# Storing two output tiles with one DMA in place of four, all on the sync queue

## The chip, the cores and the metric

The kernel runs on one core of a Trainium2 chip. The metric is the device time of one execution in microseconds (us), taken outside the profiler's page; the span that a profile shows is some 1.8 us shorter. Lower is better. Runs of one kernel scatter by about 2%; a run more than 1.5% above the fastest of its kernel is called slow. Medians below are over all runs, slow ones too; ratios are over fast runs alone.

## The reference

```python
def sm_attn(qq, kk, vv):
    s = scale * np.matmul(qq, kk.transpose(0, 1, 3, 2))
    a = np.exp(s - np.max(s, axis=-1, keepdims=True))
    a = a / (np.sum(a, axis=-1, keepdims=True) + 1e-09)
    return np.matmul(a, vv)
p_packed = sm_attn(p, k, v)              # q, k, v: (8, 8, 576, 64); p: (8, 8, 32, 64)
attn = sm_attn(q, p_packed, p_packed)
x = attn.transpose(0, 2, 1, 3).reshape(8, 576, 512)
W_tok = scale * np.einsum('bsd,btd->bst', x @ w_q, x @ w_k)
out = np.maximum(np.einsum('bst,btd->bsd', W_tok, x), 0.0) @ w_out     # (8, 576, 512) fp32
```

## The kernel before

Everything is written out as a fixed order of steps for each engine. Loads of q, k and v (fp32 in memory, bf16 on chip) go through the GpSimd queue, but for the k of the first batch, which the scalar and sync queues carry. An output tile has 128 rows: partition `s * 32 + g` holds token `18 * g + 8 * tp + 2 * s + e`, where `e` tells the two tiles of a pair apart. So for one `s`, 32 partitions hold 32 rows of memory that are 18 tokens apart, and with both tiles of a pair each of them writes 4 KB in one piece. The old code issues one DMA for each `s`:

```python
        o = new("o", (b, tp), [P, 2, D], fp32, "o", opool)          # five buffers
        copy(eng, o[:, t % 2, x:x + w], T["ot", b, t, x])
        done[b, tp] = done.get((b, tp), 0) + w
        if done[b, tp] == 2 * D:
            dst = out[b].rearrange("(g r) n -> g (r n)", r=RQ)[:, tp * 4096:(tp + 1) * 4096]
            for s in range(4):
                queue = nc.scalar if w < D and s % 2 else nc.sync   # scalar: last pair alone
                queue.dma_start(dst[:, s * 1024:(s + 1) * 1024],
                                o[s * GQ:(s + 1) * GQ].rearrange("a e n -> a (e n)"))
```

A remainder of 64 rows for two batches goes out in one DMA (`o_rem`), on the sync queue, the last one on the GpSimd queue.

The softmax here doesn't subtract the row's maximum and nothing guards it: scores larger than these inputs give would overflow.

## Time and profile before

| | before |
|---|---|
| time, median | 124.64 us (123.6 to 126.11, 3 runs, before the change was timed) |
| span of the profiled run | 122.5 us |
| PE busy | 106.5 us, 87% |
| mean DMA rate (as counted on landing) | 208 GB/s |
| output stores | 64 of 128 KB, 4 remainders of 256 KB |
| last load landed | 91.5 us |
| last output tile evacuated | 113.45 us |

The prediction shows the lines of the page that carry this. In those of section 2 (slices) each digit is a fortieth of the span, in tenths of busy time. In the table by stretches, a row is the stretch, its length, the busy time of each engine with the number of instructions, then the TensorE clock granted, the DMA share and GB/s. The DMA queues q0 and q1 carry the loads of the GpSimd queue and the DMAs of the sync queue.

### The profile page before, as it was taken

Reading aid. Unit: us, or ns where it says so; the run is one execution under the profiler, and the core shown is the slowest. Engines: PE = TensorE matmul, PEld = TensorE weight load, DVE = VectorE, ACT = ScalarE, POOL = GpSimd, SP = SyncE. Lnnn points to the kernel's source line nnn. Section 1 sums busy time; section 2 is a strip of 40 time slices with the busy share of each in tenths; the row PEclk is TensorE's granted clock in tenths of the full one; section 3 lists DMA queues with packets and bytes.
Section 4 is the critical chain, followed back from the end, with each engine's and each line's share of the span. In section 5 each row is a group of like instructions: output and inputs, shape, how many; then the busy total and the mean of one; then the engine's idle time right before and its main releaser. Section 6 shows DMA issues by size and latency. Waiting matters only on the chain.

```text
span 122.5 us, 4561 instructions
## 1 busy us (share of the span) xinstructions
PE 106.5 (87%) x1968; PEld 70.1 (57%) x1968; DVE 81.3 (66%) x197; ACT 78.2 (64%) x159; POOL 37.9 (31%) x49
## 2 busy tenths in 40 slices
PE   6989989687999999999998999989999989998000
PEld 2576746565748757568585657766585646354000
DVE  6362456667876858598864689987996988754000
ACT  3131568766779798799858888678767866464000
POOL 6949302722059004757000066600070120000200
PEclk9999999999999999999999999999999999999755
DMA  3999999999999999999999999999972526782584
GB/s 67 373 157 186 195 213 206 209 207 206 213 208 211 269 298 217 243 212 262 303 224 208 220 289 283 267 274 273 202 157 79 130 64 185 213 211 67 152 226 135
DMA packets 16485, 25.47 MB, mean 208 GB/s; under 512 B 3168, under 2 KB 11360, under 8 KB 16464
## 3 DMA queue, kind: packets, MB, share of 16 engines
q0 software_dynamic: 11872, 14.68, 68.9%
q1 hardware_dynamic: 4224, 9.64, 25.7%
q10 hardware_dynamic: 368, 0.85, 2.6%
q8 instruction: 15, 0.25, 0.7%
q14 instruction: 6, 0.05, 0.1%
HBM read 30.15 MB, written 9.44 MB: 323 GB/s over the span
## 4 chain that ended last, share of the span: by engine, by line
PE 52%; issue 16%; DVE 11%; DMA 7%; POOL 4%; ACT 3%; POOLq 1%; ACTq 0%
PE out_ps L518 14%; DMA q_sb<-in_q_dram 7%; PE qT_ps L369 6%; PE pv_ps L328 6%; PE aT_ps L423 3%; PE kT_ps L280 3%; PE e_ps L310 3%; PE e_ps L388 3%; PE mix_ps L486 2%; PE wkq_ps L444 2%; DVE kT L134 2%; DVE a L414 2%; DVE rs L404 2%; POOL wqk L169 2%; PE wkq_ps L439 2%
## 5 line engine op out<-in xcount | busy, mean ns | idle before, releaser
L414 POOL TENSOR_TENSOR a<-e,rr 128x512 bf16<-128x512 f32 (+1 forms) x12 | 15.0, 1258 | 55.2 <-DVE rr L408 34.0
L518 PE MATMUL out_ps<-wout,relu 128*128 128x512 bf16 (+1 forms) x132 | 31.4, 373 | 0.0
L518 PEld LDWEIGHTS <-relu 128*128 128x128 bf16 x132 | 11.7, 98 | 10.6 <-issue 0.4
L130 ACT ACTIVATE o<-out_ps 128x512 f32<-128x512 f32 (+1 forms) x21 | 12.3, 587 | 5.5 <-PE out_ps L518 3.8
L316 ACT ACTIVATE e<-e_ps 128x512 bf16<-128x512 f32 (+1 forms) x24 | 11.0, 490 | 7.1 <-PE e_ps L310 7.0
L404 DVE TENSOR_REDUCE rs<-e 128x16 f32<-128x512 f32 (+1 forms) x16 | 12.9, 809 | 3.2 <-ACT e L397 2.7
L397 ACT ACTIVATE e<-e_ps 128x512 f32<-128x512 f32 (+1 forms) x24 | 11.5, 524 | 4.3 <-PE e_ps L388 4.0
L134 DVE COPY o<-out_ps 128x512 f32<-128x512 f32 (+1 forms) x12 | 8.0, 664 | 5.9 <-PE out_ps L518 4.9
L496 ACT ACTIVATE relu<-mix_ps 128x512 bf16<-128x512 f32 x19 | 10.3, 600 | 1.7 <-PE mix_ps L486 1.1
L498 DVE TENSOR_SCALAR relu<-mix_ps 128x512 bf16<-128x512 f32 x13 | 8.6, 682 | 3.3 <-PE mix_ps L486 3.3
L369 PE MATMUL qT_ps<-idb,q_sb 128*64 128x128 bf16 x288 | 10.7, 220 | 0.1
L130 ACT ACTIVATE qT<-qT_ps 128x1024 bf16<-128x1024 bf16 (+1 forms) x13 | 9.3, 736 | 0.3 <-PE qT_ps L369 0.3
L559 PE MATMUL warm_ps<-warm 128*128 128x512 bf16 x26 | 8.5, 463 | 1.2 <-DVE warm L137 1.2
L369 PEld LDWEIGHTS <-q_sb 128*64 128x64 bf16 x288 | 8.7, 110 | 1.2 <-issue 0.7
L130 ACT ACTIVATE kT<-kT_ps 128x1024 bf16<-128x1024 bf16 (+2 forms) x10 | 7.3, 755 | 2.1 <-PE kT_ps L286 2.1
L388 PE MATMUL e_ps<-ppT,qT 128*128 128x64 bf16 x160 | 7.8, 193 | 0.8 <-issue 0.5
L423 PE MATMUL aT_ps<-idb,a 128*128 128x128 bf16 x80 | 7.3, 220 | 1.4 <-issue 0.7
L328 PE MATMUL pv_ps<-v_sb,e 64*64 64x192 bf16 x288 | 8.3, 246 | 0.0
L388 PEld LDWEIGHTS <-qT 128*128 128x128 bf16 x160 | 6.4, 98 | 3.0 <-issue 1.8
L134 DVE COPY qT<-qT_ps 128x1024 bf16<-128x1024 bf16 (+1 forms) x11 | 6.6, 603 | 2.1 <-PE qT_ps L369 2.1
L310 PE MATMUL e_ps<-pdiag,kT 128*64 128x64 bf16 x288 | 7.6, 197 | 0.4 <-DVE kT L134 0.2
L444 PE MATMUL wkq_ps<-aT,pqk 128*128 128x256 bf16 (+1 forms) x64 | 7.7, 233 | 0.0
(84 smaller groups left out, 192.5 us busy)
## 6 DMA issues: line engine op xcount, KB each, us to landing
out_dram<-o SPq DMA_DIRECT2D x62, 128.0 KB, 4.7
q_sb<-in_q_dram POOLq DMA_DIRECT2D x8, 576.0 KB, 15.2
v_sb<-in_v_dram POOLq DMA_DIRECT2D x8, 576.0 KB, 15.7
k_sb<-in_k_dram POOLq DMA_DIRECT2D x7, 576.0 KB, 17.1
out_dram<-o_rem SPq DMA_DIRECT2D x3, 256.0 KB, 5.9
k<-in_k_dram ACTq DMA_DIRECT2D x1, 576.0 KB, 4.3
k<-in_k_dram SPq DMA_DIRECT2D x1, 576.0 KB, 6.9
wout<-in_moe_w_out_dram POOLq DMA_DIRECT2D x2, 256.0 KB, 19.9
```

The costliest lines, as they stand in the source:

```text
L130: nc.scalar.activation(o, i, COPY)
L134: nc.vector.tensor_copy(o, i)
L310: nc.tensor.matmul(ps[halves(i), at[0]:at[1] + 1:at[1] - at[0]], T["kT", b][:, place(b, m), halves(i)], rhs, start=True, stop=True)
L316: nc.scalar.activation(e1[:, 2 * z0:2 * z1], T["s1", b, c], EXP, scale=scale)
L328: nc.tensor.matmul(T["pv", b][i][halves(cc)], lhsT, rhs, start=n == 0, stop=n == R - 1, skip_group_check=True)
L369: nc.tensor.transpose(ps[halves(x), z - z0], q_in[b][:, x, r * Dh:(r + 1) * Dh], idb)
L388: nc.tensor.matmul(ps[:, t - 2 * c, i, cc], lhsT, T["ppT", b][:, i, cc], start=True, stop=True)
L397: nc.scalar.activation(e2(b, min(c, 1))[:, o:o + n], T["s2", b, c].rearrange("a t i c (x l) -> a (t i c x) l", l=L), EXP, scale=scale)
L404: e.tensor_reduce(rs, T["e2", (b, d)], axis=AX, op=ADD)
L414: e.tensor_tensor(a2[:, 2 * d:2 * d + n].rearrange("a t i (u l) -> a (t i u) l", l=L), T["e2", (b, d)], T["rr", (b, d)].to_broadcast((P, n ...
L423: nc.tensor.transpose(ps[:, i, t - 2 * c], T["a2", b][:, t, i], idb)
L518: nc.tensor.matmul(ps, lhsT, wout[:, j, x:x + w], start=j == 0, stop=j == NJ - 1)
```

## The change

The intent: fewer, larger transfers, and no stores on the scalar queue. One DMA takes all 128 partitions of a tile pair. The 128 partitions lie in memory as 4 groups (`s`) of 32 rows (`g`), so the destination is written by hand as a pattern of three sizes, 4, 32 and 1024.

```diff
+    def store(o, b, r0, n):
+        d = out[b].rearrange("(g r) n -> g (r n)", r=RQ)[0:1, r0 * D:r0 * D + 1]
+        dst = bass.AP(d.tensor, d.offset, [[2 * D, 4], [RQ * D, GQ], [1, n * D]])
+        nc.sync.dma_start(dst, o)
+
...
         if done[b, tp] == 2 * D:
-            dst = out[b].rearrange("(g r) n -> g (r n)", r=RQ)[:, tp * 4096:(tp + 1) * 4096]
-            for s in range(4):
-                queue = nc.scalar if w < D and s % 2 else nc.sync
-                queue.dma_start(dst[:, s * 1024:(s + 1) * 1024],
-                                o[s * GQ:(s + 1) * GQ].rearrange("a e n -> a (e n)"))
+            store(o.rearrange("a e n -> a (e n)"), b, tp * 8, 2)
```

## The prediction

> **What bounds the kernel now.** I read the page first (the slices, then the DMA part), then the table by stretches of time, then the DMA view of two stretches, and last the timeline and the waits of the sync queue at the end. The slices:
>
> ```profile
> span 122.5 us, 4561 instructions
> ...
> PE   6989989687999999999998999989999989998000
> ...
> DMA  3999999999999999999999999999972526782584
> ```
>
> PE looks like the bound, 87% busy. But the DMA row is at its top from the second slice to the thirtieth, about 91 us, and only then falls. The table by stretches (the last two columns are the DMA share and GB/s) says it more sharply:
>
> ```profile
> 37.00:52.00 15.00, 14.41 (x299) 10.10 (x298) 10.50 (x28) 12.89 (x26) 6.31 (x8) 1.00 1.16 248
> ...
> 70.00:80.00 10.00, 9.64 (x190) 6.54 (x185) 9.57 (x20) 7.81 (x17) 6.18 (x6) 1.00 1.14 279
> 80.00:91.50 11.50, 11.21 (x250) 7.93 (x250) 10.05 (x26) 8.79 (x19) 2.48 (x2) 1.00 1.04 225
> 91.50:100.00 8.50, 8.50 (x134) 5.06 (x131) 6.78 (x18) 6.35 (x14) 1.05 (x1) 1.00 0.39 102
> ```
>
> The share is over 1 until 91.5 us (packets overlap a little in an engine), then 0.39: until then the 16 DMA engines have no spare time. The loads also arrive just in time. In the trace v of batch 6 landed at 80.7 us and its first matmul ran at 81.6; k of batch 7 at 85.89 and 85.93; q at 88.69 and 88.73; v at 91.5 and 91.7. The schedule had been fitted to the arrival of the loads, so the chain of waits shows PE; the rate of the DMA engines sets the pace behind it.
>
> How fast they are, from the DMA view of 70 to 80 us and from the page:
>
> ```profile
> q0 software_dynamic: 920, 1.21, 69.1%
> q1 hardware_dynamic: 558, 1.55, 43.3%
> ...
> HBM read 30.15 MB, written 9.44 MB: 323 GB/s over the span
> ```
>
> q0 carries the loads and counts what lands, which is bf16; the fp32 source is twice that. So 2 x 1.21 + 1.55 = 3.97 MB moved in 10 us: 397 GB/s. The same sum over 37 to 52 us (2.37 and 1.31 MB) gives 403. I take 400 GB/s for 16 engines, **25 GB/s for one**.
>
> The end is a different stage. PE is done at 113.0 us, but the span goes on for 9 us (timeline, then the waits of the sync queue):
>
> ```profile
> 113.07 0.38 ACT L130 ACTIVATE o<-out_ps 128x256 f32<-128x256 f32 x1 [0.65 <-PE out_ps L518]
> 113.49 0.83 ACTq L538 DMA_DIRECT2D out_dram<-o  x2
> ...
> 115.49 4.34 SPq L538 DMA_DIRECT2D out_dram<-o  x8
> ```
>
> ```profile
> SPq L538 <- DMA out_dram<-o: 7.8, 5, 5.4
> ```
>
> The sync queue stood for 5.4 us, from 110.0 to 115.49, until one of its eight completion semaphores was free. The built program's waits say which: the third store of batch 6's first tile pair waits for a semaphore that was given to one of the two stores on the scalar queue, the last of the program. That one lands at 115.47. Then eight stores are still to be issued.
>
> **What the Trainium skill says.** "DMA: Bandwidth & Descriptors", section "Why a DMA increments its semaphore by 16 and not by 1": a DMA is spread over k engines, k being the largest number up to 16 that divides the size of the slowest dimension of both access patterns, as the instruction carries them; on a sync or scalar queue they are the lowest-numbered k. For four stores before, the DMA view of 95 to 99 us has:
>
> ```profile
> DMA packets 192, 0.52 MB, mean 131 GB/s; under 512 B 64, under 2 KB 64, under 8 KB 192
> ...
> out_dram<-o SPq DMA_DIRECT2D x4, 128.0 KB, 2.1
> ```
>
> 64 small packets for four stores are 16 completions for each: k is 16, as the rule has it for 32 rows on both sides. No DMA of the kernel before has a slowest dimension that isn't a multiple of 16, so the trace doesn't test smaller k. Same page, "Specifications": about 27 GiB/s per engine; the 25 GB/s here are a little under. Same page, "Queues, rings and completion order": an engine takes turns between its queues by packets, so loads and stores on one engine slow each other. The trace doesn't show whose turn it is, but a store that lands in 2.1 us alone takes a median 6.8 us between 70 and 80 us, beside loads.
>
> **The change part by part.** It removes 64 stores of 128 KB and adds 16 of 512 KB. The bytes and the 4 KB runs are the same. The instructions of PE, ACT, DVE and POOL stay in their order.
>
> 1. Issues. 64 issues at a median 0.42 us become 16, some 20 us less of the queues' time. None of it is on the path before the tail, because there the queue waits for tiles (39.2 us for DVE and 21.6 us for ACT in the waits of the sync queue), not the tiles for the queue. Gain before 109 us: 0.
>
> 2. The tail's wait. With no store on the scalar queue, the build has no sync store waiting for a later one. The 5.4 us wait goes, and six of the eight issues after it.
>
> 3. The engines. The destination pattern of the new store is built by hand, with sizes 4, 32 and 1024; the source has 128 partitions. The build leaves it so. The largest divisor of 128 and 4 up to 16 is 4: **each new store runs on four engines, always the same four.** The old ones, 32 against 32, ran on sixteen. The remainder stores (64 rows) stay on sixteen.
>
> Bytes for each of these four engines: loads 30.15 MB / 16 = 1.884; remainder stores 4 x 0.262 / 16 = 0.066; tile stores 64 x 0.131 = 8.39 MB / 4 = 2.097. Sum 4.05 MB, at 25 GB/s **162 us of work**. Before it was (30.15 + 9.44) / 16 = 2.47 MB, 99 us, which fits engines full until 91 us and partly used after.
>
> Can they be idle in between? Per batch they have 3.54 MB of loads / 16 = 0.221 MB (8.8 us), two stores (10.5 us) and half a remainder (0.3 us): 19.6 us, against 106.5 / 8 = 13.3 us of PE. Loads are issued ahead by up to four buffers and stores queue behind up to five output buffers, so compute waits for DMA and some work is always queued. After the last load lands, compute of the last batch takes 91.7 to 113.5, some 22 us; four stores of 5.2 us cover it, and the queue should hold about as many. So hardly any idle time. The loads need all sixteen engines to be complete, hence the other twelve can't help: they only wait.
>
> Sum: 162 us of work; 2.5 us in which the engines start (the first slice of 3 us moves 67 GB/s); 2 us from the last packet's end to the end of the span (landing 0.9 us before it in this trace, receipt about 1); 1.8 us from span to time (124.31 against 122.5). **168 us**, 43 us more than now. The 5.4 us of part 2 are gained and can't be seen, as the end is set by the four engines' backlog.
>
> **The rivals.**
>
> *Sixteen engines anyway* (the queue splits by partitions, whatever the destination). For it: no run here shows a k under 16. Against it: the rule is stated for the pattern as carried. Then only part 2 counts: the last tile is ready at 113.45; issue 0.55 us (what the remainder stores took); 512 KB at 400 GB/s 1.3 us; fixed part 1.8 us (128 KB landed in 2.1 us, 0.3 of it transfer); 0.9 to the end: 118 us of span, about 120 us of time, 4% faster.
>
> *Four engines, but hidden in the middle,* so that only the tail shows it. Then the last three stores (ready at 109.3, 111.6, 113.5) follow each other at 5.2 us: 109.8 + 15.6 = 125.4, with receipt 1.8 and 0.9 us a span of 128, about 130 us: 4% slower. The DMA share over 1 for 80 us speaks against it: there's nowhere to hide 60 us.
>
> *Fewer, larger transfers gain by themselves,* as the same page's "Rules for kernel authors" advises to coalesce small ones. It would show where fixed costs of stores are on the path; here stores of 128 KB are pipelined eight deep, and 4 KB packets stay 4 KB. Worth nothing before the tail.
>
> **Range and chances.** That k is 4 I hold for about 0.88. Given that, the time is bytes over rate: at 408 GB/s (loads alone, 20 to 25 us: 1.02 MB landed, twice that read) 160 + 4 = 164 us or a little less; with a poorer mix of two queues, or waits that the in-order GpSimd queue adds when its loads are held back, 5 to 15 us more. I keep 154 to 184. Of the rest, 0.09 is for sixteen engines (faster) and 0.03 for something that cancels.
>
> **What would show it.** Right: about 4 small packets for a store in a stretch with stores alone, in place of 16; a store's landing at some 7 us alone and far more when queued; a mean DMA share falling to about half with some engines full; loads landing later, 20 us and more, and DVE, ACT or PE waiting for loads and for output stores; PE busy about 106 us of a span of 166. Wrong: stores landing in about 3.5 us at 16 completions each and a span near 118 (first rival), or loads landing as before to 91 us and only the tail longer (second).

## More of the kernel before

For the inputs that are drawn, the rows (tokens) of one batch of the output are nearly equal: worked out from the reference, values go up to 1.5e-4 and no row differs from the mean row of its batch by more than 1.1e-9. The comparison with the reference therefore can't see rows that are stored in the wrong place.

One more view is needed for later, the list of DMA issues of the kernel before: tiles, queue, count, size and the median time from issue to landing.

```profile
out_dram<-o SPq DMA_DIRECT2D x62, 128.0 KB, 4.7
q_sb<-in_q_dram POOLq DMA_DIRECT2D x8, 576.0 KB, 15.2
v_sb<-in_v_dram POOLq DMA_DIRECT2D x8, 576.0 KB, 15.7
k_sb<-in_k_dram POOLq DMA_DIRECT2D x7, 576.0 KB, 17.1
```

Loads take a median 15 to 17 us, with several queued at a time; the DMA share is over 1 while they are.

## The result, and the profile after

The changed kernel took **171.68 us** (median, 170.71 to 173.66, 4 runs), beside 124.14 us for the kernel before (now 4 runs). The ratio is 1.3823 (95% interval 1.3693 to 1.3953). Ratios in this document are the mean time of one kernel's fast runs over that of the other's of the same rounds, so they are not quite the ratio of the medians quoted. The profiled run took 170.71 us.

The slices of the changed kernel, a fortieth being 4.2 us here:

```profile
span 168.9 us, 4478 instructions
...
PE   7999849799899394673874881964699996100000
...
PEclk9999999999999879998799696599999999855555
DMA  5999999999999999522239884222212422422221
GB/s 159 261 205 213 205 208 208 209 213 207 237 239 246 237 236 234 129 83 73 80 83 203 210 170 106 78 83 67 91 54 52 139 105 95 146 108 100 106 103 45
```

The reader sees three stages. Up to the sixteenth slice (68 us) the DMA row is as full as before. PE already has gaps there that it had not before (a 3 and a 4 in the fourteenth and sixteenth slice). Then the DMA row, which before stayed at 9, falls to between 1 and 5, but for three slices around 95 us, when new loads go out: mostly a quarter of the engines' time. PE has more gaps in that stage. In the last five slices nothing computes at all and the DMA row stays at 2.

The table by stretches, read like that of before:

```profile
37.00:60.00 23.00, 19.77 (x389) 13.70 (x391) 14.93 (x38) 17.34 (x34) 11.37 (x12) 0.96 1.15 232
60.00:80.00 20.00, 12.74 (x277) 9.27 (x274) 7.97 (x18) 9.08 (x20) 0.00 (x0) 0.93 0.67 149
...
100.00:120.00 20.00, 12.16 (x235) 8.51 (x234) 9.40 (x23) 8.39 (x18) 2.48 (x2) 0.83 0.37 93
...
155.00:168.90 13.90, 0.00 (x0) 0.00 (x0) 0.00 (x0) 0.00 (x0) 0.00 (x0) 0.50 0.21 86
```

Before, PE was busy for 9.64 of the 10 us from 70 to 80; here for 12.74 of the 20 us from 60 to 80. Now the DMA view of a stretch at the end where stores run alone (155 to 165 us), and of one in the middle (70 to 80 us):

```profile
DMA packets 261, 1.04 MB, mean 104 GB/s; under 512 B 8, under 2 KB 8, under 8 KB 261
...
q1 hardware_dynamic: 261, 1.04, 25.3%
```

```profile
q1 hardware_dynamic: 133, 0.53, 13.9%
q0 software_dynamic: 173, 0.24, 13.5%
```

At the end, 1.04 MB are two stores, with 8 small packets: **4 completions for a store, where there were 16**. The share is 25.3%, which is 4 engines of 16, and the rate 104 GB/s, 26 for each of the four. Stores are queued there, so if each store went to another four engines, several would run side by side and the share would be higher, unless the queue worked them off one at a time. The DMAs that run on all sixteen engines settle it, by the sixteen steps of their semaphores in the trace. Before, the last load of v (issued at 79.04 us) has its steps from 88.99 to 91.52. In the changed kernel it was issued at 96.61 and has twelve steps from 102.06 to 102.45, but the last four from 120.01 to 121.81; the remainder store issued at 132.36 has twelve by 136.07 and four from 139.32 to 142.27. So it is always the same four engines. In the middle, loads (0.24 MB landed, 0.48 read) and stores (0.53) share the four engines almost evenly: 1.01 MB in 10 us, 101 GB/s again. The other twelve engines have done their part of the loads, as those steps show, and have nothing to do.

What waits for that (from the waits, then the chain that ended last, then the DMA issues):

```profile
PE pv_ps L328 <- DMA v_sb<-in_v_dram: 11.3, 4, 4.1
...
PE kT_ps L280 <- DMA k_sb<-in_k_dram: 4.8, 2, 3.5
...
DVE o L134 <- DMA out_dram<-o: 4.1, 1, 4.1
```

```profile
DMA 37%; PE 24%; issue 13%; DVE 5%; POOL 3%; ACT 3%; POOLq 0%
```

Before, DMA had 7% of that chain and PE 52%:

```profile
PE 52%; issue 16%; DVE 11%; DMA 7%; POOL 4%; ACT 3%; POOLq 1%; ACTq 0%
```

```profile
out_dram<-o SPq DMA_DIRECT2D x16, 512.0 KB
q_sb<-in_q_dram POOLq DMA_DIRECT2D x8, 576.0 KB, 23.4
v_sb<-in_v_dram POOLq DMA_DIRECT2D x8, 576.0 KB, 22.3
k_sb<-in_k_dram POOLq DMA_DIRECT2D x7, 576.0 KB, 19.8
```

Loads land after a median 20 to 23 us in place of 15 to 17, but the worst take twice that. For v, before and after:

```profile
DMA to landing us min/median/max: 10.1/15.7/23.9
```

```profile
DMA to landing us min/median/max: 8.8/22.3/47.0
```

The last load lands at 121.8 us in place of 91.5. The last tile is evacuated at 144.6 us in place of 113.45: 31 us later. From there to the end of the span it takes 24 us in place of 9: 15 more. Together these are the 46 us that the span grew.

That the store has no landing time has a cause that tells something. The profile looks for 16 steps of the semaphore for each DMA. In the trace's records of the semaphores, a store issued at 125.62 us has five: one at 126.57, then 133.71, 133.88, 135.64 and 136.75. That fits what the Trainium skill, "DMA: Bandwidth & Descriptors", section "Why a DMA increments its semaphore by 16 and not by 1", says of a DMA on k engines: the issuing sequencer writes the missing 16 - k at once, then each of the k engines adds one as its data has landed.

### The profile page after: what moved, and what is told of

Read it like the earlier page. It is cut to its first block, busy times and chain, and to the rows that moved or that the text cites. A ratio compares the mean times of both kernels' runs of the same rounds, so it can differ in the third digit from the quotient of the medians.

```text
span 168.9 us, 4478 instructions
## 1 busy us (share of the span) xinstructions
PE 112.4 (67%) x1952; PEld 74.3 (44%) x1968; DVE 82.1 (49%) x197; ACT 78.8 (47%) x159; POOL 37.9 (22%) x49
## 4 chain that ended last, share of the span: by engine, by line
DMA 37%; PE 24%; issue 13%; DVE 5%; POOL 3%; ACT 3%; POOLq 0%
DMA k_sb<-in_k_dram 22%; DMA v_sb<-in_v_dram 15%; PE warm_ps L561 4%; PE out_ps L518 4%; PE pv_ps L328 3%; PE kT_ps L286 2%; PE qT_ps L369 2%; POOL a L414 2%; PE e_ps L310 1%; PE aT_ps L423 1%; PE kT_ps L280 1%; PE px_ps L253 1%; PE e_ps L388 1%; DVE rs L404 1%; DVE kT L134 1%
## 5 line engine op out<-in xcount | busy, mean ns | idle before, releaser
L518 PE MATMUL out_ps<-wout,relu 128*128 128x512 bf16 (+1 forms) x122 | 30.7, 378 | 0.5
L328 PE MATMUL pv_ps<-v_sb,e 64*64 64x192 bf16 x288 | 9.4, 272 | 11.3 <-DMA v_sb<-in_v_dram 11.3
L404 DVE TENSOR_REDUCE rs<-e 128x16 f32<-128x512 f32 (+1 forms) x16 | 12.9, 809 | 3.6 <-ACT e L397 3.2
L496 ACT ACTIVATE relu<-mix_ps 128x512 bf16<-128x512 f32 x19 | 10.3, 600 | 8.9 <-issue 5.5
L328 PEld LDWEIGHTS <-e 64*64 64x64 bf16 x288 | 6.9, 119 | 14.1 <-DMA v_sb<-in_v_dram 8.5
L134 DVE COPY kT<-kT_ps 128x1024 bf16<-128x1024 bf16 (+1 forms) x13 | 7.1, 556 | 5.8 <-PE kT_ps L280 4.4
L444 PE MATMUL wkq_ps<-aT,pqk 128*128 128x256 bf16 (+1 forms) x64 | 8.5, 249 | 0.0
```

Source lines behind the costliest of these rows:

```text
L134: nc.vector.tensor_copy(o, i)
L328: nc.tensor.matmul(T["pv", b][i][halves(cc)], lhsT, rhs, start=n == 0, stop=n == R - 1, skip_group_check=True)
L404: e.tensor_reduce(rs, T["e2", (b, d)], axis=AX, op=ADD)
L496: nc.scalar.activation(o, i, RELU)
L518: nc.tensor.matmul(ps, lhsT, wout[:, j, x:x + w], start=j == 0, stop=j == NJ - 1)
```

## The experiments

My theory: the loss is that each new store runs on the same four engines, because its pattern's slowest size is 4. Rival A: few large stores are worse than many small ones. Rival B: the hand-written pattern of three sizes is slow to generate. Rival C: one queue in place of two costs something. A second question was where the expected gain of the queue change went.

### All tile stores on the sync queue, else as before

```diff
-                queue = nc.scalar if w < D and s % 2 else nc.sync
+                queue = nc.sync
```

> Edit: the kernel before with its two scalar-queue stores put on the sync queue too; still 64 stores of 128 KB, 32 rows each. Theory (the loss is the four engines; the queue half of the change is a gain that the loss hides): the wait of 5.4 us on a later store's semaphore goes. Last tile ready at 113.4, up to four issues at 0.47 us, 2.1 us to land, 0.9 to the end: span about 118, time about 120 us, 0.96 to 0.97 of before. Rival (one queue is what costs): slower than before, part of the 47 us appears here.

Measured: 122.9 us (121.78 to 124.24, 4 runs) beside 124.85 of before; ratio 0.9829 (0.9724 to 0.9933). Rival C falls: one queue costs nothing, it gains a little (the interval leaves out 1). The wait of 5.4 us is gone. But I had expected 120 us. In the trace the tile stores were all landed at 118.4 us; the last remainder, on the GpSimd queue, landed at 117.9, and the span ended 2.1 us after that, at 120.0. In the kernel before, the span ended 1.0 us after the last store on the sync queue. So here another store sets the end, which had been hidden.

### The sizes of the pattern exchanged

```diff
-        dst = bass.AP(d.tensor, d.offset, [[2 * D, 4], [RQ * D, GQ], [1, n * D]])
+        dst = bass.AP(d.tensor, d.offset, [[RQ * D, GQ], [2 * D, 4], [1, n * D]])
```

Rows land permuted. Bytes, rows, runs of 4 KB, number of DMAs and queue stay as in the changed kernel.

> Edit: the changed kernel with the destination pattern's first two sizes exchanged (32, 4 in place of 4, 32), so the result is wrong on purpose; 16 stores of 512 KB, same rows, same bytes, same queue. Theory (four engines because the slowest dimension is 4): 16 engines a store, 16 small packets a store, loads as early as before, span about 118 and time about 120 us. Rival A (few large stores are bad by themselves: coarse, land late) : remains near 170 us. Rival B (hand-made three-size pattern is slow to generate): remains near 170 us.

Measured: 124.14 us. One line with two sizes exchanged takes away nearly the whole loss. It was 4 us more than expected, and its start had been late, so it was timed again:

> The same kernel as the run with reordered sizes, timed in rounds: its one look began 2 us late (first output tile evacuated at 37.4 us, against 34.8 and 35.1 in two others), before any store was issued. If that is chance of the start, the median is 121 to 123 us, 0.97 to 0.99 of before; if one large store costs something itself, it stays near 124.

Measured: **122.71 us** (122.35 to 122.88, 4 runs), ratio 0.9878 (0.9789 to 0.9967). The profiled run of these began late too (first output tile from 36.6 us), so that the late start was chance is not shown. In the DMA view of one store that runs alone (98 to 101 us):

```profile
DMA packets 144, 0.52 MB, mean 175 GB/s; under 512 B 16, under 2 KB 16, under 8 KB 144
...
out_dram<-o SPq DMA_DIRECT2D x1, 512.0 KB, 3.0
```

Sixteen completions, 128 packets of 4 KB, and 3.0 us from issue to landing. Rivals A and B fall: a large store in a pattern of three sizes is quick when the slowest size is 32. It is also about as quick as four small ones: this kernel and the one with all tile stores on sync differ only in that, and they took 122.7 and 122.9 us. They were timed in different rounds, and in both the remainder on the GpSimd queue sets the end (here it landed at 118.9 us, 0.7 after the last tile store), so a difference of 1 us or so would not show.

### Small stores on four engines

```diff
-                queue = nc.scalar if w < D and s % 2 else nc.sync
-                queue.dma_start(dst[:, s * 1024:(s + 1) * 1024],
-                                o[s * GQ:(s + 1) * GQ].rearrange("a e n -> a (e n)"))
+                d = dst[0:1, s * 1024:s * 1024 + 1]
+                d = bass.AP(d.tensor, d.offset, [[RQ * D, 4], [4 * RQ * D, GQ // 4], [1, 1024]])
+                nc.sync.dma_start(d, o[s * GQ:(s + 1) * GQ].rearrange("a e n -> a (e n)"))
```

> Edit: the kernel before, all stores on the sync queue, each still 128 KB of 32 rows, but the 32 rows are named as 4 times 8, the 4 outermost (rows land permuted: wrong on purpose). Theory: four engines a store again, whatever its size: 162 us of work on those four, time about 168 to 174 us. Rival A (the size of the store): like before, about 120 to 124 us.

Measured: 170.22 us. In a stretch of 25 us near the end (140 to 165), the queue line is that of four engines again:

```profile
q1 hardware_dynamic: 705, 2.53, 25.0%
```

So 64 stores of 128 KB on four engines cost as much as 16 of 512 KB on four, and 16 of 512 KB on sixteen as little as 64 of 128 KB on sixteen. The size of the store plays no part that these times show; the spread is what counts.

### Two engines and eight

The first is a right result: two stores of 64 partitions each, destination sizes 2, 32 and 1024. The second is the edit above with 8 in place of 4.

> Edit: two stores of 256 KB (64 partitions, destination 2, 32, 1024) for each two tiles; a right result. Theory: the slowest sizes are 64 and 2, so two engines a store: loads and remainders 1.95 MB on each, tile stores 8.39 / 2 = 4.19 MB, 6.14 MB at 25 GB/s = 246 us, and 6 us as in the prediction: about 252 us (240 to 265). Rival (large stores land late, so smaller ones are better): between 122 and 171 us, as the size is between.

Measured: 245.14 us, beside the expected 252. From 225 to 240 us, where stores run alone, they have a DMA share of 12.9%: two engines of 16.

> Edit: 64 stores of 128 KB, the 32 rows named as 8 times 4 (rows land permuted). Theory: eight engines: 1.95 + 8.39 / 8 = 3.00 MB at 25 GB/s = 120 us, and 6 us: about 126 us, up to 133 because such a kernel is at the edge where compute and the eight engines are both nearly full. Rival (the three-size pattern itself is slow): near the 170 us of 4 times 8.

Measured: 132.96 us, at the upper end of what was expected. In the trace's records a store has nine steps of its semaphore, one for the missing half and eight landings.

| engines a store | work on those engines, at 25 GB/s | sum with 6 us | measured |
|---|---|---|---|
| 2 | 246 us | 252 | 245.1 |
| 4 | 162 us | 168 | 171.7 (170.2 small) |
| 8 | 120 us | 126 | 133.0 |
| 16 | 99 us | not the bound | 122.9 and 122.7 |

The time follows the bytes on the busiest engines. It's 3% under the sum at two engines, where those are by far the bound, 2% over it at four and 6% over it at eight. That at eight it is over because engines and compute are both nearly full was expected, but no run shows it apart.

### The wait at the end, brought back

All tile stores on the sync queue, the last remainder on the scalar queue.

```diff
-            queue = nc.gpsimd if b == B - 1 else nc.sync
+            queue = nc.scalar if b == B - 1 else nc.sync
...
-                queue = nc.scalar if w < D and s % 2 else nc.sync
+                queue = nc.sync
```

> Edit: all 64 tile stores on the sync queue, but the last remainder store on the scalar queue (before: the GpSimd queue). The build gives it a semaphore that a sync store of batch 6 waits for. Theory (the 5.4 us at the end of the kernel before were such a wait): the wait comes back: the sync queue stands from about 110.5 until that store has landed, about 116, then nine issues of 0.45 us and 2.1 us to land: time about 124 to 126 us, 2 to 4 more than with all tile stores on sync. Rival (the scalar queue was only slow to issue): 121 to 122 us.

Measured: 125.83 us. In the waits of the sync queue:

```profile
SPq L538 <- DMA out_dram<-o_rem: 5.0, 1, 5.0
```

The sync queue's issues stop at 112.2 us; the remainder is issued at 114.8 and lands at 117.25; the next sync issue, which belongs to an earlier batch, starts at 117.27. One DMA on the other queue, given a semaphore of the common eight in an order that isn't the order in time, stops the whole queue. In the kernel before it was the same: the sync issue at 115.49 us waited for the semaphore of the scalar queue's store of 113.49, which landed at 115.47.

### A version that beats both

All tile stores and all remainders on the sync queue, stores still of 32 rows:

```diff
-            queue = nc.gpsimd if b == B - 1 else nc.sync
+            queue = nc.sync
...
-                queue = nc.scalar if w < D and s % 2 else nc.sync
+                queue = nc.sync
```

> Edit: all tile stores and all remainder stores on the sync queue, still 32 rows each; a right result, wanted as a version that beats both. In the run with only the tile stores on sync, the remainder on the GpSimd queue landed at 117.9 us, and the span went on to 120.0; the sync stores landed at 118.4. On sync it is issued 17th in the tail, at about 115.6, and lands at about 119: span 119.9 to 120.2, so within 1 us of that run: about 122 us, 0.98 of before.

Measured: **120.6 us** (119.73 to 121.82, 6 runs), ratio to before 0.9722 (0.9651 to 0.9792). That is 2.8% faster than the kernel before and the fastest; its interval overlaps that of the tile stores alone (0.9724 to 0.9933). The last DMA lands at 117.04 us and the span ends at 117.96, so the 2.1 us after the GpSimd queue's store are down to 0.9.

### One store on sixteen engines with the rows in their right places

The exchanged sizes are right if partition `4 * g + s` holds what partition `32 * s + g` held. The relu step can write its tile in that order, with a step of four elements. The destination has the exchanged sizes, as above, and:

```diff
-        relu(eng, o, T["mx", b, j])
+        relu(eng, o.rearrange("a (t g s) -> a t s g", g=GQ, s=4),
+             T["mx", b, j].rearrange("a (t s g) -> a t s g", g=GQ, s=4))
```

> Edit: the changed kernel with the token order inside a tile turned (relu written with a stride, so that partition p is group p//4, row pair p%4) and the destination 32, 4, 1024: a right result with one store of 512 KB on sixteen engines. Theory: about 120 us like the run with reordered sizes, or some us more if the strided writes of relu (32 of them, 0.60 and 0.68 us each) get longer. Rival A: near 170 us.

Measured: 131.1 us (129.83 to 131.56, 4 runs), ratio 1.0482 (1.0368 to 1.0597). Again not near 170, so the spread is what counts, but worse than before. Groups of instructions (line, engine, operation, shapes, count, then busy us and the mean ns of one), first of the kernel before, then of this run:

```profile
L496 ACT ACTIVATE relu<-mix_ps 128x512 bf16<-128x512 f32 x19 | 10.3, 600 | 1.7 <-PE mix_ps L486 1.1 <-ACT o L130 0.3 <-ACT aT L130 0.2
L498 DVE TENSOR_SCALAR relu<-mix_ps 128x512 bf16<-128x512 f32 x13 | 8.6, 682 | 3.3 <-PE mix_ps L486 3.3
```

```profile
L496 ACT ACTIVATE relu<-mix_ps 128x512 bf16<-128x512 f32 x19 | 23.3, 1369 | 1.3 <-PE mix_ps L486 0.7 <-ACT o L130 0.3 <-ACT aT L130 0.2
L498 DVE TENSOR_SCALAR relu<-mix_ps 128x512 bf16<-128x512 f32 x13 | 16.3, 1301 | 2.7 <-PE mix_ps L486 2.7
```

The writes with a step took 1369 and 1301 ns, against 600 and 682 before. In busy time that is 13.0 us more on ACT and 7.7 us more on DVE. The edit also cuts 512 elements in a row into 16 runs of 32; no run tells the step from the runs. Against the exchanged sizes without it (122.7) it cost 8.4 us. Four plain stores are the better way to sixteen engines here.

### Where the loss arises: late stores alone, early stores alone

The store of the changed kernel for some batches, four stores of 32 rows for the others, all on the sync queue:

```diff
+            if b > 4:          # and, in the other run: b < 5
+                store(o.rearrange("a e n -> a (e n)"), b, tp * 8, 2)
+            else:
+                ...            # four stores of 32 rows on nc.sync
```

> Edit: the changed kernel's one store of 512 KB only for batches 5 to 7 (the last six of sixteen), four stores of 32 rows on the sync queue for batches 0 to 4; a right result. Theory: loads land as in the kernel before (about 91 us), since these six are ready only after that (from 100 us); the six follow each other on the four engines at 5.2 us: 100.5 + 31.4 = 132, with 1.8 and 0.9 to the end and 1.8 from span to time about 136 us (132 to 139). This is the drain's part of the 47 us: about 14 over the 122.9 of all tile stores on sync. Rival (the loss comes with the loads alone): 123.

Measured: 143.44 us, 20.5 over the 122.9 of all tile stores on sync. I had said 14. The loads were as early as before (last at 92.0 us), and the last stores did follow each other quickly: they landed at 119.3, 125.2, 130.2, 135.2 and 140.1, the last four 5.0 us apart. But the first of the six, issued at 101.5, landed only at 111.8: 10.3 us, not 7. The 4 KB packets of stores took a mean 229 ns in that stretch (100 to 110 us) against 159 at the end, and they came with gaps between them.

> Edit: the reverse: one store of 512 KB for batches 0 to 4 (ten of sixteen), four of 32 rows for batches 5 to 7; a right result. Theory: the four engines share loads with those stores; in the changed kernel the last load landed at 121.8 us and the last tile was evacuated at 144.5; the same here, then a tail on sixteen engines of some 6 us: time about 152 us (147 to 157), 29 over 122.9: the loads' part. With the drain's part of 14 that makes 43 of about 48. Rival (only the backlog at the end costs): 123.

Measured: 155.57 us, 32.7 over 122.9; 29 was expected. The last load landed at 124.2 us. So about 33 us come from loads held back and 20 from the drain at the end, 53 together, where the changed kernel lost 48.8 against the same base. That the sum is 4 us too large may be overlap of the two parts, but each is one run, so this is not shown.

## Why the prediction was right

It said 168 us with 154 to 184; measured was 171.68.

- **What bounds it.** That the DMA engines, not PE, set the pace until 91 us was right: as soon as four of them had more to do, every later load and matmul was late, though PE's own work stayed nearly the same. (The DMA row is at its top up to the twenty-ninth slice, not the thirtieth, which stands at 7; nothing rests on that.)
- **Part 1, issues.** Worth nothing, as predicted: one large store and four small ones on sixteen engines took 122.7 and 122.9 us.
- **Part 2, the wait at the end.** The reading of the cause was right: it went with the scalar queue's stores and came back with another DMA there (5.0 us). Its worth was smaller at first than the 5.4 us: 1.7% (ratio 0.9829), as the GpSimd queue's remainder set the end next. With that moved too it was 2.8% (ratio 0.9722), and 120.6 us. The first rival's figure for sixteen engines, about 120 us, was reached only so, and with small stores: with the GpSimd queue's remainder at the end, which the prediction had not in its sum, it was 122.7, and the gain 1.2% in place of 4%. In the changed kernel the wait is gone as well, but the four engines' backlog ends far later.
- **Part 3, the engines.** k is 4: shown by four completions a store, by a share of 25.3%, and by the exchange of two sizes that undoes the loss. Always the same four: shown by loads and remainders of which twelve engines are done long before the other four (by 35 us for the load of v that was issued at 57.77 us). The 25 GB/s for one engine were 25.2 in the middle (101 / 4) and 26 at the end (104 / 4). The prediction called 25 GB/s a little under the skill's 27 GiB/s; that is 29 GB/s, so it is 14% under.
- **The sum.** 162 us of work and 4.5 us around it gave a span of 166.5; it was 168.9. Two terms were off in opposite ways. A store that finds the four engines empty takes 10 to 11 us to land, not 5.2 and 1.8 (101.5 to 111.8 in the run with late stores, 125.6 to 136.75 in the changed kernel), and there are some such gaps: "hardly any idle time" was a little too good. In the queue, a store takes 5.0 us, a little less than 5.2. That they nearly cancel is luck: at 26 GB/s the 4.05 MB would be 156 us (an estimate), 6 us under the sum, and some 8 us of idle or slow time make it up.
- **A slip in the range.** At 408 GB/s the work is 159 us, and with the 6 us of the sum 165, not 160 + 4.
- **The second rival** (four engines, hidden in the middle, 130 us) fell: 30 us of the loss come from the loads, as the last landing at 121.8 us shows. The third rival (larger transfers gain by themselves) fell with part 1.
- **Signs that were wrong in size.** A store alone was to land in some 7 us (10 to 11), and the mean DMA share was to be about half; the queues' shares add up to 68%, where it was 98% before. I had also named "PE busy about 106 us" as a mark. It was 112.4. The same matmuls ran longer, for instance those of line 328 272 ns in place of 246. The granted clock was 0.83 on average from 100 to 120 us, where it had been 1.00 throughout the loads before: PE waits more, and is slower afterwards. The Trainium skill, "TensorE: Matmul & The Clock Gate", section "Part 1: The HAM clock gate", says that after some 3.4 us without work the array falls back to half its clock; this trace agrees roughly. The clock was 0.50 in the idle tail, and also from 58.2, 78.7 and 92.4 us for over 3 us and from 102.6 for 6.7, each time during or soon after a pause of PE of 2.5 to 4.1 us.

What stays open: why the first 4 KB packets of a 512 KB store on four idle engines are slow (229 ns on average, with gaps), when those of one on sixteen take 160 ns. It is not the number of engines alone: in the traces, 4 KB packets of the old 128 KB stores, alone on sixteen engines, took 253 ns too (95 to 99 us of the kernel before), and those of 128 KB stores on four, in the queue, 161. No run here separates the engines' start from their choice of partitions.

## What to carry to other kernels

Before merging several DMAs into one, write down the outermost size of both patterns as the instruction will carry them. On the sync queue here, the largest number up to 16 that divides both, not the bytes, decided how many DMA engines worked, and it was always the same ones. If a change leaves most of them out, compute the bytes on the busiest engine, over the rate that the trace shows for one; here this gave the time within 6% for two, four and eight engines. And where two queues share completion semaphores, look in the built program for an early DMA that waits for a late one.

## What the Trainium skill lacked or had wrong

- "DMA: Bandwidth & Descriptors", "Rules for kernel authors": its advice to coalesce small transfers puts the overhead under 64 KB, and from 128 KB up it gained nothing here by itself (64 of 128 KB: 122.9 us; 16 of 512 KB on sixteen engines: 122.7 us). Coalescing over an outermost size of 4 cost 47 us; of that the page does warn, in its rule on the spread, which held at 2, 4, 8 and 16 engines, and again in the row "Use all 16 engines" of the same table, so there it lacked nothing.
- Same page, "Why a DMA increments its semaphore by 16 and not by 1": gives no duration for small k. A store of 512 KB on four engines landed 5.0 us after the one before it when queued, but took 10.3 and 11.1 us when issued to idle engines; on sixteen it took 3.0 us.
- No page that I read has it: two queues that share a set of completion semaphores can stop each other. A sync store waited 5.4 us (kernel before) and 5.0 us (brought back) for a later DMA on the scalar queue.
- No page that I read has it: with the last store on the GpSimd queue the span ended 2.1 us after its landing, with it on the sync queue 0.9 us.
- "SBUF — State Buffer", "Door 1: The DMA port swizzle": its note on 16-byte lines says that bf16 can be stepped by up to 8 elements for free. Writes of bf16 with a step of 4 took 1369 ns on ACT and 1301 on DVE, against 600 and 682 without a step; as the edit also makes the runs shorter, that the step alone costs this is not shown.
